# Sixteen chunks of score products split between TensorE and VectorE, and the softmax bias moved from GpSimd to ScalarE, in a two-layer decode kernel

## The chip, the cores and the metric

The kernel runs on one core of one Trainium2 chip. The metric is the device time of one execution in microseconds (us), smaller is better. Engines are named as in the profile: PE is TensorE, PEld its weight load, DVE is VectorE, ACT is ScalarE, POOL is GpSimd, SP is the engine that issues DMA transfers. L882 is line 882 of the kernel that the trace belongs to. All runs told of here gave correct results by the reference's tolerance and were in the fast state.

## The reference, cut to what matters

Two layers, each attention over a key/value cache followed by a small mixer MLP, for one new token of each of two sequences.

```python
B, Sq, D = 2, 1, 576;  H, Sk, Dh = 32, 16384, 128;  F = 4608      # all bf16
def A(x):                                    # attention
    q = (x @ wq).reshape(B, Sq, H, Dh).transpose(0, 2, 1, 3)
    scores = einsum("bhqd,bhkd->bhqk", q, k_cache) * Dh ** -0.5
    p = softmax(scores)
    return einsum("bhqk,bhkd->bhqd", p, v_cache)... @ wo
def B(x):                                    # MLP
    h  = gelu(layernorm(x) @ w1)
    hs = concatenate(shifted slices of h) @ w2     # every slice is shifted along S
    x1 = x + hs
    return x1 + gelu(layernorm(x1) @ w3) @ w4
for _ in range(2):
    x = x + A(layernorm(x));  x = x + B(layernorm(x))
```

With S = 1 every shift leaves zeros, so h is never used: the kernels compute it and multiply w2 by a zero tile. The weight of the problem is the cache: 64 pairs of batch and head, 4 MB of K and 4 MB of V each, read once per layer. I call one pair a unit; there are 128 units in a run.

## The kernel before: the parts that matter

A unit's 16,384 keys are 128 blocks of 128 keys, in 16 chunks of 8 blocks. K lies with the keys on the partitions, and the kernel's score matmul takes it with the head's 128 elements there, so each block is first transposed on TensorE into PSUM, copied to SBUF by VectorE or (every third chunk) ACT, and then used as the weights of a matmul with one column of q.

```python
def pe_transposes(pe, u, c):                 # chunk c of unit u
    ...
    for i in range(CH):                      # CH = 8
        ins = pe.transpose(self.tps[slot][:, i*128:(i+1)*128], self.kbuf[kslot][:, jj, :], self.ident)   # L808
def copy_chunk(eng, g, is_act):              # is_act for every third chunk
    ...
    if is_act: ins = eng.activation(out=self.ktsb[:, ks], in_=src, func=ACT.Copy)      # L863
    else:      ins = eng.tensor_copy(out=self.ktsb[:, ks], in_=src)                    # L866
def pe_scores(pe, g):
    ...
    for i in range(CH):
        ins = pe.matmul(self.sps[sb][:, j:j+1], lhsT=self.ktsb[:, ks, i], rhs=self.qt_sb[:, gu:gu+1], ...)  # L831
```

When a unit's scores are there, the softmax follows across four engines, and the product with V last:

```python
def dve_rowmax(dv, ul): ...                  # max along the free axis -> m_sb                       L873
def pool_allreduce(g_, ul):
    self.wt(g_, "sem_rmax", gu + 1)
    g_.partition_all_reduce(self.mall_sb[:, gu:gu+1], self.m_sb[:, gu:gu+1], channels=128, reduce_op=ROP.max) # L879
    self.wt(g_, "sem_pool", gu + 1)
    g_.tensor_scalar(out=self.bias_sb[:, gu:gu+1], in0=self.mall_sb[:, gu:gu+1], scalar1=-scale, ...)         # L882
def act_exp(act, ul):
    self.wt(act, "sem_bias", gu + 1)
    ...
    act.activation(out=self.p_sb[pb], in_=self.sps[sb][:, 0:NB], func=ACT.Exp,
                   bias=self.bias_sb[:, gu:gu+1], scale=scale, accum_out=self.l_sb[:, gu:gu+1])               # L892
def pe_pv(pe, ul): ...                       # 128 matmuls of V blocks with columns of p             L847
```

K and V come in halves of 2048 KB, two of each per unit, into four K slots and five V slots; each is asked for when its slot comes free.

## Time and profile before

| | before |
|---|---|
| median of the first 6 runs | 3765.46 us (3756.93 to 3771.26) |
| span of the traced run | 3765.6 us |
| busy: PE, DVE, ACT, POOL | 62%, 26%, 20%, 2% |
| DMA, mean over the span | 298 GB/s |
| one unit | 28.2 us |

The prediction below shows the busy shares, the chain and the three idle times that carry the argument. Three more lines complete them. From the page of the kernel before, the queue that carries K and V (packets, MB, share of the time of 16 DMA engines) and the largest group of instructions (busy us, mean ns | idle before):

```profile
q1 hardware_dynamic: 96520, 1116.54, 74.6%
...
L808 PE MATMUL tps<-ident,kbuf 128*128 128x128 bf16 x16384 | 1698.9, 267 | 22.7 <-issue 19.0
```

A quarter of the DMA's time is unused, and the transposes are by far the costliest work. A reader who stops here will want to take transposes off TensorE. The view of the one source line of the bias says otherwise (duration min/median/max, first and last start):

```profile
L882 POOLq MODIFY_POOL_CONFIG  x256: 82/83/85, 40.9 to 3699.9; - x128
L882 POOL TENSOR_SCALAR bias_sb<-mall_sb x128: 260/260/262, 48.6 to 3707.1; 128x1 f32<-128x1 f32 x128
```

The bias is 128 instructions of 0.26 us; in front of each stand two changes of the GpSimd's configuration of 0.08 us. The changes themselves look free. The first one starts at 40.9 us and the bias it belongs to at 48.6: what costs is the time after them, which no instruction shows. The gap is 11.0 us on average and lies between 7.06 and 14.02. The prediction and the expectations call such a change, with the gap behind it, a code change. That is my name for it: what GpSimd does in the gap no trace shows.

For the sums of the prediction the trace gives three times on VectorE: a reduce of 360 inputs takes 532 ns (L682), one of 320 takes 492 ns (L641), so 1 ns per input and some 170 ns fixed, and a copy of 1024 elements out of PSUM takes 692 ns (L866). It holds no multiply of the size that the change brings, so the prediction's times for that are my estimate; the measured ones stand with the result.

### The profile page before, as it was taken

Reading aid. Unit: us, or ns where it says so; the run is one execution under the profiler, and the core shown is the slowest. Engines: PE = TensorE matmul, PEld = TensorE weight load, DVE = VectorE, ACT = ScalarE, POOL = GpSimd, SP = SyncE. Lnnn points to the kernel's source line nnn. Section 1 sums busy time; section 2 is a strip of 40 time slices with the busy share of each in tenths; the row PEclk is TensorE's granted clock in tenths of the full one; section 3 lists DMA queues with packets and bytes.
Section 4 is the critical chain, followed back from the end, with each engine's and each line's share of the span. In section 5 each row is a group of like instructions: output and inputs, shape, how many; then the busy total and the mean of one; then the engine's idle time right before and its main releaser. Section 6 shows DMA issues by size and latency. Waiting matters only on the chain.

```text
span 3765.6 us, 107964 instructions
## 1 busy us (share of the span) xinstructions
PE 2324.8 (62%) x50634; PEld 2280.1 (61%) x50634; DVE 988.3 (26%) x1646; ACT 762.0 (20%) x962; POOL 88.1 (2%) x279
## 2 busy tenths in 40 slices
PE   5556666656656656656665665566566656566566
PEld 5556666656656656656555655566566656566565
DVE  2222222222222222222232222222222222222222
ACT  2112112212122112112121211221122122121121
POOL 0000000000000000000000000000000000000000
PEclk8666666666766666666566666666666666666675
DMA  9777776877777777777497877678777777777774
GB/s 399 314 291 290 303 316 273 319 317 304 312 294 294 305 298 291 297 308 292 167 414 293 318 297 304 272 294 318 297 295 301 291 297 313 308 289 306 302 292 151
DMA packets 96965, 1123.44 MB, mean 298 GB/s; under 512 B 8964, under 2 KB 28680, under 8 KB 28680
## 3 DMA queue, kind: packets, MB, share of 16 engines
q1 hardware_dynamic: 96520, 1116.54, 74.6%
q8 instruction: 397, 6.50, 0.7%
q14 instruction: 48, 0.39, 0.0%
HBM read 1116.51 MB, written 0.00 MB: 297 GB/s over the span
## 4 chain that ended last, share of the span: by engine, by line
PE 48%; issue 42%; ACT 4%; POOL 2%; DVE 2%; DMA 1%; POOLq 0%; ACTq 0%; SPq 0%
PE tps L808 27%; PE ops L847 11%; PE sps L831 8%; ACT ktsb L863 3%; POOL mall_sb L879 1%; DVE m_sb L873 1%; POOL bias_sb L882 1%; ACT p_sb L892 1%; DMA wring<-in_B_w_dram 1%; PE tps L506 1%; DVE ktsb L866 0%; DMA kbuf<-in_A_k_cache_dram 0%; PE mps L506 0%; PE sps L666 0%; POOLq L882 0%
## 5 line engine op out<-in xcount | busy, mean ns | idle before, releaser
L808 PE MATMUL tps<-ident,kbuf 128*128 128x128 bf16 x16384 | 1698.9, 267 | 22.7 <-issue 19.0
L866 DVE COPY ktsb<-tps 128x1024 bf16<-128x1024 bf16 x1366 | 931.7, 692 | 2594.1 <-PE tps L808 2591.8
L831 PE MATMUL sps<-qt_sb,ktsb 128*128 128x1 bf16 x16384 | 763.1, 167 | 1288.1 <-ACT ktsb L863 1264.2
L831 PEld LDWEIGHTS sps<-qt_sb,ktsb 128*128 128x128 bf16 x16384 | 730.4, 106 | 1315.5 <-ACT ktsb L863 1289.9
L808 PEld LDWEIGHTS tps<-ident,kbuf 128*128 128x128 bf16 x16384 | 1288.1, 120 | 28.3 <-issue 23.1
L863 ACT ACTIVATE ktsb<-tps 128x1024 bf16<-128x1024 bf16 x682 | 697.2, 1022 | 1107.9 <-PE tps L808 1107.9
L847 PE MATMUL ops<-p_sb,vbuf 128*128 128x1 bf16 x16384 | 443.1, 163 | 60.8 <-issue 42.9
L847 PEld LDWEIGHTS ops<-p_sb,vbuf 128*128 128x128 bf16 x16384 | 429.9, 97 | 65.5 <-issue 47.5
L892 ACT ACTIVATE p_sb<-sps,bias_sb 128x128 bf16<-128x128 f32 x128 | 47.0, 368 | 1776.0 <-POOL bias_sb L882 1776.0
L879 POOL PARTITION_ALL_REDUCE mall_sb<-m_sb x128 | 48.8, 382 | 2136.7 <-DVE m_sb L873 2136.7
L882 POOL TENSOR_SCALAR bias_sb<-mall_sb 128x1 f32<-128x1 f32 x128 | 33.3, 260 | 1411.7 <-issue 1411.7
L873 DVE TENSOR_REDUCE m_sb<-sps 128x1 f32<-128x128 f32 x128 | 36.4, 284 | 39.8 <-PE sps L831 39.7
L892 ACT ACTIVATION_READ_ACCUMULATOR p_sb<-sps,bias_sb 128x1 f32 x128 | 24.7, 193 | 0.0
L506 PE MATMUL tps<-gT_bf,wring 128*128 128x2 bf16 x288 | 19.2, 171 | 5.3 <-DVE gT_bf L395 3.7
L506 PE MATMUL tps<-otn_sb,wring 128*128 128x2 bf16 x256 | 17.1, 171 | 7.1 <-DVE otn_sb L727 7.1
L624 PE MATMUL sps<-xn,wring 128*128 128x2 bf16 (+1 forms) x320 | 9.3, 165 | 18.4 <-DVE xn L361 13.0
L624 PEld LDWEIGHTS sps<-xn,wring 128*128 128x128 bf16 (+1 forms) x320 | 8.9, 104 | 18.8 <-DVE xn L361 13.2
L337 ACT ACTIVATE rstd<-var,epsb 128x2 f32<-128x2 f32 x8 | 2.4, 296 | 83.3 <-DVE var L330 83.3
L506 PEld LDWEIGHTS tps<-gT_bf,wring 128*128 128x128 bf16 x288 | 13.3, 108 | 7.2 <-DVE gT_bf L395 3.9
L506 PEld LDWEIGHTS tps<-otn_sb,wring 128*128 128x128 bf16 x256 | 11.9, 108 | 8.2 <-DVE otn_sb L727 7.3
L506 PE MATMUL mps<-gT_bf,wring 128*64 128x2 bf16 x72 | 15.1, 210 | 0.0
L666 PE MATMUL sps<-xn,wring 128*128 128x2 bf16 (+1 forms) x360 | 10.1, 165 | 7.4 <-DVE xn L361 7.4
(80 smaller groups left out, 110.7 us busy)
## 6 DMA issues: line engine op xcount, KB each, us to landing
kbuf<-in_A_k_cache_dram SPq DMA_DIRECT2D x256, 2048.0 KB, 8.4
vbuf<-in_A_v_cache_dram SPq DMA_DIRECT2D x256, 2048.0 KB, 15.9
wring<-in_B_w_dram SPq DMA_DIRECT2D x12, 864.0 KB, 8.9
wring<-in_A_wo_dram SPq DMA_DIRECT2D x8, 1152.0 KB, 19.3
wring<-in_B_w_dram SPq DMA_DIRECT2D x8, 1152.0 KB, 5.4
wring<-in_A_wq_dram SPq DMA_DIRECT2D x8, 1024.0 KB, 9.7
wring<-in_B_w_dram SPq DMA_DIRECT2D x6, 576.0 KB, 5.5
wring<-in_A_wq_dram SPq DMA_DIRECT2D x2, 512.0 KB, 14.3
```

Of the source, the lines that this page charges most:

```text
L506: ins = pe.matmul(self.out_bank(t), lhsT=wap[0:kk, t * 128:t * 128 + kl], rhs=rhs_fn(k), start=(k == 0), stop=(k == nk - 1))
L624: ins = pe.matmul(parts[:, k * U + h * B:k * U + (h + 1) * B], lhsT=wap[0:kk, h * 128:(h + 1) * 128], rhs=self.xn[0:kk, k, :], start=True, ...
L666: ins = pe.matmul(parts[:, k * MB + m * B:k * MB + (m + 1) * B], lhsT=wap[0:kk, m * 128:(m + 1) * 128], rhs=self.xn[0:kk, k, :], start=Tru ...
L808: ins = pe.transpose(self.tps[slot][:, i * 128:(i + 1) * 128], self.kbuf[kslot][:, jj, :], self.ident[:, :])
L831: ins = pe.matmul(self.sps[sb][:, j:j + 1], lhsT=self.ktsb[:, ks, i, :], rhs=self.qt_sb[:, gu:gu + 1], start=True, stop=True)
L847: ins = pe.matmul(self.ops_[:, gu:gu + 1], lhsT=self.vbuf[vslot][:, jj, :], rhs=self.p_sb[pb][:, j:j + 1], start=(j == 0), stop=(j == NB - 1))
L863: ins = eng.activation(out=self.ktsb[:, ks, :, :], in_=src, func=ACT.Copy)
L866: ins = eng.tensor_copy(out=self.ktsb[:, ks, :, :], in_=src)
L873: dv.tensor_reduce(out=self.m_sb[:, gu:gu + 1], in_=self.sps[sb][:, 0:NB], axis=AX.X, op=ALU.max).then_inc(self.sems["sem_rmax"], 1)
L879: g_.partition_all_reduce(self.mall_sb[:, gu:gu + 1], self.m_sb[:, gu:gu + 1], channels=128, reduce_op=ROP.max).then_inc(self.sems["sem_po ...
L882: g_.tensor_scalar(out=self.bias_sb[:, gu:gu + 1], in0=self.mall_sb[:, gu:gu + 1], scalar1=-scale, scalar2=None, op0=ALU.mult).then_inc(se ...
L892: act.activation(out=self.p_sb[pb][:, :], in_=self.sps[sb][:, 0:NB], func=ACT.Exp, bias=self.bias_sb[:, gu:gu + 1], scale=scale, accum_out ...
```

## The change

Its intent is to take most of the transposes, copies and score matmuls off TensorE. Chunks 0 to 5 of each unit stay there. The other ten (80 blocks) are computed by VectorE: K, keys on partitions, times q in every partition, summed along the free axis. On the way the bias goes to ACT, exp splits in two (scores in PSUM, scores in SBUF), the two denominators are added once per layer on GpSimd, and the unused h branch moves to the layer's end. The core of the diff, cuts marked:

```diff
 def pool_allreduce(g_, ul):
     g_.partition_all_reduce(self.mall_sb[...], self.m_sb[...], channels=128, reduce_op=ROP.max)
-    self.wt(g_, "sem_pool", gu + 1)
-    g_.tensor_scalar(out=self.bias_sb[...], in0=self.mall_sb[...], scalar1=-scale, ...)
 def act_exp(act, ul):
+    self.wt(act, "sem_pool", gu + 1)
+    act.activation(out=self.bias_sb[...], in_=self.mall_sb[...], func=ACT.Copy, scale=-scale)
     self.wt(act, "sem_bias", gu + 1)
-    act.activation(out=self.p_sb[pb][:, :], in_=self.sps[sb][:, 0:NB], func=ACT.Exp, ..., accum_out=self.l_sb[...])
+    act.activation(out=self.p_sb[pb][:, 0:NBP],  in_=self.sps[sb][:, 0:NBP],   func=ACT.Exp, ..., accum_out=self.l_sb[...])
+    act.activation(out=self.p_sb[pb][:, NBP:NB], in_=self.s_dve[sb][:, 0:NBD], func=ACT.Exp, ..., accum_out=self.l2_sb[...])
+def dve_diag(dv, ul): ...      # ident * q  -> diag_sb
+def pe_qb(pe, ul): ...         # ones^T @ diag: q in every partition, PSUM
+def dve_qb_copy(dv, ul): ...   # -> qb_sb
+def dve_dots(dv, ul, h):       # the blocks of K half h that are VectorE's
+    kap = self.kbuf[kslot][:, jj0:jj0 + nblk, :]
+    qb_bc = bass.AP(..., ap=[partition, [0, nblk], row of 128])
+    dv.tensor_tensor(out=kap, in0=kap, in1=qb_bc, op=ALU.mult)
+    dv.tensor_reduce(out=self.s_dve[ss][:, ...], in_=kap, axis=AX.X, op=ALU.add)
+    dv.tensor_copy(out=self.junk1[...], in_=self.ident[:, 0:1])        # then frees the K half
 ... (row maximum of both parts; the K slot is free when both engines are done with it)
 def attn_normalize(self, l):
+    g.tensor_tensor(out=self.l_sb[...], in0=self.l_sb[...], in1=self.l2_sb[...], op=ALU.add)   # GpSimd, once per layer
     g.partition_all_reduce(self.den_sb[...], self.l_sb[...], channels=128, reduce_op=ROP.add)
 ... (w1, its layer norm and gelu: moved behind the end of the layer)
-KB(..., NKB=4, NVB=5, NW=5)
+KB(..., NKB=4, NVB=5, NW=5, NKT=4, NCP=6, ACT_COPY_EVERY=1)           # NCP: chunks left on TensorE
```

> **What bounds the kernel now.** I read the page's busy shares first, then the groups with their idle times, then the chain of waits over one unit, then the DMA rate by window. A unit is one batch and head: 128 of them, 64 in each of two layers. No engine is full:
>
> ```profile
> PE 2324.8 (62%) x50634; PEld 2280.1 (61%) x50634; DVE 988.3 (26%) x1646; ACT 762.0 (20%) x962; POOL 88.1 (2%) x279
> ...
> PE 48%; issue 42%; ACT 4%; POOL 2%; DVE 2%; DMA 1%; POOLq 0%; ACTq 0%; SPq 0%
> ...
> L831 PE MATMUL sps<-qt_sb,ktsb 128*128 128x1 bf16 x16384 | 763.1, 167 | 1288.1 <-ACT ktsb L863 1264.2
> ...
> L892 ACT ACTIVATE p_sb<-sps,bias_sb 128x128 bf16<-128x128 f32 x128 | 47.0, 368 | 1776.0 <-POOL bias_sb L882 1776.0
> ...
> L882 POOL TENSOR_SCALAR bias_sb<-mall_sb 128x1 f32<-128x1 f32 x128 | 33.3, 260 | 1411.7 <-issue 1411.7
> ```
>
> The reader is to see a chain of three idle times with the same count of about 128. TensorE waits 1264 us for an ACT copy; ACT stands 1776 us behind an exp that waits for the bias; the bias, a 0.26 us GpSimd multiply, starts after 1411.7 us of "issue", 11.0 us each time (1411.7 / 128). The chain of waits over one unit shows it in order:
>
> ```profile
> 1003.14 0.38 POOL mall_sb L879
> 1003.52 0.07 POOLq L882 x2
> 1003.59 11.35 issue
> 1014.94 0.27 POOL bias_sb L882
> ...
> 1015.70 0.92 ACT ktsb L863
> 1016.62 0.05 issue
> 1016.66 0.38 PE sps L831 x8
> ```
>
> The two queue entries in front of the gap are, in the view of that source line, MODIFY_POOL_CONFIG, 256 of them in the run[...]. Behind the late bias ACT, in order, holds up one copy out of PSUM, TensorE's score matmuls wait for that copy, and all stops for 11 to 12 us per unit.
>
> The first attention stretch runs from 26.8 us to the end of its last PV at 1833.2 us, the second from 1900.8 to 3711.5 us: 28.2 us per unit. TensorE is busy in only 16.5 us of such a unit, and so is the DMA for three quarters of it:
>
> ```profile
> 1000.00:1028.10 28.10, 16.54 (x391) 16.37 (x389) 6.98 (x11) 6.49 (x8) 0.64 (x2) 0.74 0.76 304
> ```
>
> ```profile
> 22.00:32.00 10.00, 9.78 (x243) 9.74 (x244) 3.51 (x8) 1.12 (x2) 0.00 (x0) 1.00 0.99 421
> 32.00:42.00 10.00, 9.63 (x232) 9.33 (x229) 6.98 (x11) 5.98 (x6) 0.38 (x1) 1.00 1.01 426
> ```
>
> The last two columns are DMA share and GB/s. With its queue full the DMA moves 421 to 426 GB/s, so 304 is no limit yet. It will be the next one.
>
> [...]
>
> **The change, part by part.** It keeps the first 6 of a unit's 16 chunks of keys on TensorE (transpose, copy, score matmul), all 6 copies now on ACT, and gives the other 10 chunks (80 blocks of 128 keys) to VectorE: multiply K in place by a broadcast q, then reduce. It moves the bias from GpSimd to ACT, splits exp in two, adds a diagonal and one matmul to broadcast q, and puts the unused h branch at the layer's end. The order of instructions shows that the GpSimd queue in a layer's loop is now 64 all-reduces and nothing else.
>
> GpSimd: 128 code changes of 11.0 us leave the loop. All of it was on the path. One pair remains per layer (a tensor_tensor on the denominators between two all-reduces), which costs what the last unit's pair costs now: 14.6 us from the all-reduce at 3699.5 to the reciprocal at 3714.1.
>
> TensorE per unit: 48 transposes and 48 score matmuls in place of 128 and 128. A chunk of both takes 0.65 us at the high clock and 1.06 us at the low one (successive transposes in the timeline), so 6 take 3.9 to 6.4 us; PV stays at 3.3 us; q's matmul 0.3 us. Sum 7.5 to 10 us.
>
> ACT per unit: 6 copies of 1.02 us, bias 0.25, two exps of about 0.3 with 0.19 for each accumulator: 7.4 us.
>
> VectorE per unit[...]: multiply of 2048 and 8192 elements[...] 1.22 and 4.42 us; reduces 2.28 and 8.68; two markers of one element 0.30; three small ops of row maximum 0.59; diagonal 0.19; copy of q from PSUM 0.28. Sum 17.96 us. Eleven gaps of 0.04 us between dependent ops (seen in the layer norm) and the trip to TensorE and back, 0.45 us, make 18.9 us. This is a serial loop: row maximum of one unit, q of the next, its dots.
>
> DMA per unit: four transfers of 2048 KB, 8.39 MB; at 424 GB/s 19.8 us.
>
> So the DMA, at 19.8, lies just above VectorE at 18.9, and TensorE and ACT are far below. Can the DMA be kept busy? The second K half is asked for when the dots of two units earlier end, and two V halves follow it at once: three transfers, 14.8 us. The first K half follows when its own dots and the sixth transpose are done, by my reckoning about 8 us later, well before those have drained. So yes.
>
> The sum. K/V of a layer: 64 x 19.8 = 1267 us, and 4.7 MB of wo in the same queue 11 us: 1278. Layer 1: K starts at 12 us, after wq; slower start (312 GB/s in 12 to 22 us) 3 us; last softmax 2 us: all-reduce at 1295; denominators to 1310. From there to the first K of layer 2, now 1835.9 to 1883.7: 48 us, so 1358. Layer 2: 1278 + 3 + 2 + 15 gives 2656. From there to the end, now 3714.1 to 3765.6: 52 us. **2708, say 2710 us.** The h branch leaves the middle of the layer but stays in order on the same engines ahead of the next norm and of the final cast, so I give it nothing.
>
> **Rivals.** (a) VectorE sets the pace: [...] Then 5.3 us more per unit, 24.2, and about 3270 us. [...] (b) VectorE's loop with its waits is nearer to 21 us, because the all-reduce, exp and q's trip add up more than I counted: about 2850. [...] (c) The gain is all from the code change that left GpSimd, and the offload to VectorE is hidden: TensorE's 16.5 us plus some 3 us of softmax wait would already sit near the DMA's 19.8. I believe this largely: it makes the same time, but says that the bias alone would bring nearly all of the gain. (d) The author's likely reason, that TensorE's transposes are the bound, gives 28.2 down to about 18.9; it makes no other time, since DMA then binds, but would leave the bias alone with little. The 11.35 us of issue speak against it.
>
> **Range and chances.** At 437 GB/s, the best rate in short slices of the trace, 1239 us per layer give about 2630. A loop of 21 us gives 2850. I take 2630 to 2850. Faster by over 2% is near certain (0.98): even (a) is faster by 13%. What is left is an unseen stall, 0.01 each.
>
> **What would show it.** In the new profile: no MODIFY_POOL_CONFIG in the loops and no 11 us issue gap before a bias; DMA share 0.95 or more at 415 to 430 GB/s through attention; multiplies of 8192 elements at 4.4 us and reduces at 8.7 us; VectorE busy about 18 us of 20 per unit, waiting for K where it waits; TensorE under half busy. A multiply of 8.7 us would be (a); DMA below 90% with VectorE never waiting for K would be (b); a code change still in the loop would break all of it.

## The result, and the profile after

The changed kernel takes 2724.86 us, the median of 8 runs (2723.14 to 2726.36), against 3761.82 us, the median of 16 runs of the kernel before. The ratio is 0.7243 (95% interval 0.7232 to 0.7255). Here and below a ratio is the mean time of one kernel's fast runs over that of the other's fast runs in the same rounds, so it is not quite the ratio of the medians quoted.

The page of the changed kernel, parts 1, 3, 4 and 5:

```profile
PE 1403.1 (52%) x30282; PEld 1358.1 (50%) x30282; DVE 2324.9 (85%) x1554; ACT 913.2 (34%) x1432; POOL 51.7 (2%) x155
...
q1 hardware_dynamic: 96520, 1116.54, 97.7%
...
DMA 66%; DVE 22%; PE 7%; issue 4%; SPq 0%; POOL 0%; ACT 0%; DVEq 0%; POOLq 0%
...
L924 PE MATMUL tps<-ident,kbuf 128*128 128x128 bf16 x6144 | 772.1, 305 | 407.7 <-DMA kbuf<-in_A_k_cache_dram 406.1
...
L978 PE MATMUL ops<-p_sb,vbuf 128*128 128x1 bf16 x16384 | 471.2, 165 | 629.5 <-DMA vbuf<-in_A_v_cache_dram 615.7
```

The bytes are the same as before; the share of DMA time that carries them rose from 74.6% to 97.7%. In the chain the 42% of issue have become 4%, and DMA, 1% before, is 66%. TensorE now waits for K and for V, not for a copy. One unit in the timeline (start us, duration us, engine, instruction, [idle before <- releaser]):

```profile
1004.55 0.35 POOL L1072 PARTITION_ALL_REDUCE mall_sb<-m_sb  x1 [19.22 <-DVE m_sb L1063]
...
1004.93 0.20 ACT L1080 ACTIVATE bias_sb<-mall_sb 128x1 f32<-128x1 f32 x1 [0.32 <-POOL mall_sb L1072]
1005.00 0.29 DVE L1015 CAST qb_sb<-mps 128x128 bf16<-128x128 f32 x1 [0.38 <-PE mps L962]
...
1005.38 1.23 DVE L1036 TENSOR_TENSOR kbuf<-kbuf,qb_sb 128x2048 bf16<-128x2048 bf16 x1
...
1006.65 2.29 DVE L1039 TENSOR_REDUCE s_dve<-kbuf 128x16 f32<-128x2048 bf16 x1
...
1009.17 4.42 DVE L1036 TENSOR_TENSOR kbuf<-kbuf,qb_sb 128x8192 bf16<-128x8192 bf16 x1
1013.63 8.69 DVE L1039 TENSOR_REDUCE s_dve<-kbuf 128x64 f32<-128x8192 bf16 x1
...
1021.03 1.03 PE L924 MATMUL tps<-ident,kbuf 128*128 128x128 bf16 x8 [3.04 <-DMA kbuf<-in_A_k_cache_dram]
...
1023.36 0.24 DVE L1052 TENSOR_REDUCE m_sb<-s_dve 128x1 f32<-128x80 f32 x1 [0.79 <-PE sps L949]
...
1024.13 0.35 POOL L1072 PARTITION_ALL_REDUCE mall_sb<-m_sb  x1 [19.23 <-DVE m_sb L1063]
```

From one all-reduce to the next are 19.58 us, against 28.2 before. This is a common unit and not the mean: after the first eight of a layer, every fourth or fifth one takes about 21 us or more, for a reason that was not looked into, and the mean of the first layer is 19.91 us ((1301.83 - 47.71) / 63, from its first and its last all-reduce). The bias starts 0.03 us after its all-reduce ends (1004.55 + 0.35 to 1004.93). VectorE is a serial loop that almost fills the unit; its longest wait here, 0.79 us, is for TensorE's scores, and TensorE had waited 3.04 us for a K half. So the DMA seems to set the pace, with VectorE right behind it; an experiment below tests that. Three of these units in the view by window (length, busy us of PE, PEld, DVE, ACT, POOL with instructions, granted clock, DMA share, GB/s):

```profile
1000.00:1060.00 60.00, 31.38 (x675) 30.47 (x675) 53.70 (x34) 21.06 (x33) 1.05 (x3) 0.56 1.01 426
```

One thing in the new trace the kernel before doesn't have. At the end of each layer's stream the DMA doesn't stop sharply. The DMA view of 1250 to 1330 us in 40 slices of 2 us:

```profile
DMA  9999999999999999999975445543000000059999
GB/s 442 434 426 418 442 426 410 385 410 434 418 434 426 434 410 434 434 426 422 387 303 221 205 205 221 205 187 129 31 0 0 0 0 0 0 115 438 406 414 419
```

All remaining V transfers had been asked for by 1272.5 us, yet the eight slices from 1290 to 1306 us have a mean of 210 GB/s, at about half of the DMA share. The packed trace says why. It keeps the times of the 16 landing signals of every transfer (no view lists them; there are 16 DMA engines). At 210 us the 16 signals of a V half come within 5 us of each other. (In the kernel before, with its DMA not full, those of the first layer's last V half come within 2 us.) For the last V half of the layer, eight come at 1289.2 to 1291.6 us and the other eight at 1303.6 to 1305.9. So half of the signals run ahead by 14 us at the end, and the tail is the other half finishing alone. That each eight belongs to eight engines is inferred; it fits the half share.

### The profile page after: what moved, and what is told of

It reads as the page before. It is cut to its first block, busy times and chain, and to the rows that moved or that the text cites. A ratio compares the mean times of both kernels' runs of the same rounds, so it can differ in the third digit from the quotient of the medians.

```text
span 2723.7 us, 66636 instructions
## 1 busy us (share of the span) xinstructions
PE 1403.1 (52%) x30282; PEld 1358.1 (50%) x30282; DVE 2324.9 (85%) x1554; ACT 913.2 (34%) x1432; POOL 51.7 (2%) x155
## 3 DMA queue, kind: packets, MB, share of 16 engines
q1 hardware_dynamic: 96520, 1116.54, 97.7%
## 4 chain that ended last, share of the span: by engine, by line
DMA 66%; DVE 22%; PE 7%; issue 4%; SPq 0%; POOL 0%; ACT 0%; DVEq 0%; POOLq 0%
DMA kbuf<-in_A_k_cache_dram 62%; DVE s_dve L1039 12%; DVE kbuf L1036 6%; DMA vbuf<-in_A_v_cache_dram 4%; PE tps L924 4%; PE sps L949 1%; DVE qb_sb L1015 1%; PE mps L962 1%; DVE diag_sb L1006 1%; DVE m_sb L1052 1%; PE tps L537 1%; DVE m_sb L1057 1%; DVE junk L1044 0%; PE mps L537 0%; DMA wring<-in_B_w_dram 0%
## 5 line engine op out<-in xcount | busy, mean ns | idle before, releaser
L1039 DVE TENSOR_REDUCE s_dve<-kbuf 128x16 f32<-128x2048 bf16 (+1 forms) x256 | 1404.4, 5486 | 8.8
L994 ACT ACTIVATE ktsb<-tps 128x1024 bf16<-128x1024 bf16 x768 | 780.6, 1024 | 1519.3 <-PE tps L924 1499.9
L924 PE MATMUL tps<-ident,kbuf 128*128 128x128 bf16 x6144 | 772.1, 305 | 407.7 <-DMA kbuf<-in_A_k_cache_dram 406.1
L924 PEld LDWEIGHTS tps<-ident,kbuf 128*128 128x128 bf16 x6144 | 593.6, 139 | 418.1 <-DMA kbuf<-in_A_k_cache_dram 416.1
L1036 DVE TENSOR_TENSOR kbuf<-kbuf,qb_sb 128x2048 bf16<-128x2048 bf16 (+1 forms) x256 | 723.3, 2825 | 12.9 <-issue 1.3
L949 PEld LDWEIGHTS sps<-qt_sb,ktsb 128*128 128x128 bf16 x6144 | 313.8, 114 | 1.5 <-ACT ktsb L994 1.4
L949 PE MATMUL sps<-qt_sb,ktsb 128*128 128x1 bf16 x6144 | 302.4, 170 | 0.6 <-ACT ktsb L994 0.5
L1052 DVE TENSOR_REDUCE m_sb<-s_dve 128x1 f32<-128x80 f32 x128 | 30.2, 236 | 145.1 <-PE sps L949 144.7
L1044 DVE CAST junk<-ident 128x1 f32<-128x1 bf16 x256 | 39.4, 154 | 27.2 <-DVE s_dve L1039 0.9
L1090 ACT ACTIVATE p_sb<-s_dve,bias_sb 128x80 bf16<-128x80 f32 x128 | 44.8, 350 | 0.0
L1086 ACT ACTIVATE p_sb<-sps,bias_sb 128x48 bf16<-128x48 f32 x128 | 38.6, 301 | 4.3
L537 PE MATMUL tps<-otn_sb,wring 128*128 128x2 bf16 x256 | 17.1, 171 | 19.9 <-DVE otn_sb L818 19.9
```

The source lines that it names most:

```text
L924: ins = pe.transpose(self.tps[slot][:, i * 128:(i + 1) * 128], self.kbuf[kslot][:, jj, :], self.ident[:, :])
L949: ins = pe.matmul(self.sps[sb][:, j:j + 1], lhsT=self.ktsb[:, ks, i, :], rhs=self.qt_sb[:, gu:gu + 1], start=True, stop=True)
L994: ins = eng.activation(out=self.ktsb[:, ks, :, :], in_=src, func=ACT.Copy)
L1036: dv.tensor_tensor(out=kap, in0=kap, in1=qb_bc, op=ALU.mult).then_inc(self.sems["sem_dotm"], 1)
L1039: dv.tensor_reduce(out=self.s_dve[ss][:, j0 - NBP:j1 - NBP], in_=kap, axis=AX.X, op=ALU.add).then_inc(self.sems["sem_dot"], 1)
L1052: i1 = dv.tensor_reduce(out=self.m2_sb[:, gu:gu + 1], in_=self.s_dve[sb][:, 0:NBD], axis=AX.X, op=ALU.max)
```

## The experiments

Each run is listed with the ratio to the kernel before of its own rounds.

| run | median us | ratio (95%) |
|---|---|---|
| the change, again, beside the next three | 2724.72 | 0.7254 (0.7237 to 0.7271) |
| before + bias on ACT | 2736.82 | 0.7287 (0.7267 to 0.7308) |
| the change without the offload | 2736.13 | 0.7284 (0.7267 to 0.7301) |
| the change with the bias on GpSimd | 2947.89 | 0.7842 (0.7817 to 0.7867) |
| the change, V transfers halved (wrong on purpose) | 2574.68 | 0.6845 (0.6823 to 0.6867) |
| before + bias on ACT, V transfers halved (wrong on purpose) | 2429.31 | 0.6458 (0.6437 to 0.6479) |
| the change, denominators added on VectorE | 2705.70 | 0.7193 (0.7175 to 0.7211) |
| the same, next layer's first K and V prefetched | 2716.15 | 0.7221 (0.7206 to 0.7236) |
| denominators on VectorE, 10 chunks on TensorE | 2717.49 | 0.7230 (0.7209 to 0.7252) |
| denominators on VectorE, 4 chunks on TensorE | 2965.15 | 0.7888 (0.7858 to 0.7918) |

The theory is rival (c) of the prediction: the gain comes from the configuration changes that left GpSimd, after which the DMA binds. Against it stands rival (d): the transposes were the bound, and the offload brings the gain. The first four runs, on one chip, are the two parts alone and together, and a control.

**The bias alone.** The kernel before, with nothing but the bias moved:

```diff
 # pool_allreduce
-    self.wt(g_, "sem_pool", gu + 1)
-    g_.tensor_scalar(out=self.bias_sb[...], in0=self.mall_sb[...], scalar1=-scale, ...)
 # act_exp
-    self.wt(act, "sem_bias", gu + 1)
+    self.wt(act, "sem_pool", gu + 1)
+    act.activation(out=self.bias_sb[...], in_=self.mall_sb[...], func=ACT.Copy, scale=-scale)
+    self.wt(act, "sem_bias", gu + 1)
```

> The kernel before with one edit: the bias is made on ACT (a Copy activation with scale) and no longer on GpSimd. Theory A (the code change on GpSimd is what the time went to, DMA is next): the 11 us issue gap goes, a unit takes the DMA's 19.6 us as it does in the changed kernel (TensorE needs 16.5 us plus about 1.5 us of softmax), DMA share near 1.0, and the layer's end saves its last code change too: 2680 to 2740 us. Theory B (TensorE's transposes are the bound, so the offload to VectorE is what pays): little changes, 3600 us or more. In between, TensorE in its serial order with the softmax wait takes more than the DMA, say 21 us a unit: 2880 us, and then the offload has a share.

Measured: 2736.82 us (2736.29 to 2737.77). Of the 1028.8 us that the whole change saves in these rounds (3753.54 - 2724.72), this one line saves 1016.7, which is 99%. From its timeline, and its view by window:

```profile
1034.90 0.35 POOL L879 PARTITION_ALL_REDUCE mall_sb<-m_sb  x1 [20.19 <-DVE m_sb L873]
1035.29 0.20 ACT L887 ACTIVATE bias_sb<-mall_sb 128x1 f32<-128x1 f32 x1 [1.41 <-POOL mall_sb L879]
```

```profile
1000.00:1060.00 60.00, 47.13 (x1139) 45.91 (x1136) 22.06 (x35) 17.59 (x25) 1.06 (x3) 0.77 1.00 424
```

The 11 us in front of the bias are gone, 0.04 us are left, and with all 256 transposes and score matmuls still on TensorE the DMA is full at 424 GB/s. TensorE, busy 47.13 of 60 us, has room. Rival (d) falls.

What fills the gap is not shown. The runs show that the gap comes and goes with the change between an all-reduce and a plain operation: 11.0 us, 128 times, in the kernel before, and none in this one's loop. The two queues of kind "instruction" moved 397 and 48 packets in the kernel before, and 397 and 44 here, so the DMA views show no traffic that goes with the 128 gaps.

**Everything but the offload.** The changed kernel with all 16 chunks on TensorE and the copies shared as before:

```diff
-KB(..., NKT=4, NCP=6,  ACT_COPY_EVERY=1)
+KB(..., NKT=4, NCP=16, ACT_COPY_EVERY=3)
```

> The changed kernel with all 16 chunks on TensorE and one copy in three on ACT, as before: everything of the change but the offload. Theory A: as the bias alone, 2680 to 2740 us, within 1% of that run; the moved h branch is worth nothing. Theory B: 3600 us or more. If the moved h branch had a price or a gain, it is the difference between this run and the bias alone.

Measured: 2736.13 us (2734.49 to 2736.94), within 0.7 us of the bias alone, with overlapping ranges. So the moved h branch, which is in this kernel and not in the other, is worth nothing that shows. (The two differ also in the buffers of transposed K, NKT=4 here and 5 there.)

**The offload without the bias.** The changed kernel with the bias back on GpSimd:

```diff
 # pool_allreduce
+    self.wt(g_, "sem_pool", gu + 1)
+    g_.tensor_scalar(out=self.bias_sb[...], in0=self.mall_sb[...], scalar1=-scale, ...)
 # act_exp
-    self.wt(act, "sem_pool", gu + 1)
-    act.activation(out=self.bias_sb[...], in_=self.mall_sb[...], func=ACT.Copy, scale=-scale)
```

> The changed kernel with the bias put back on GpSimd. Theory A: the code change is back, 11 to 14 us between all-reduce and bias; ACT's copies of chunks 2 to 5 wait behind it, TensorE's last scores come about 22 us after the row maximum before, so a unit takes 22 to 25 us: 3000 to 3400 us, and VectorE waits for TensorE's scores at the row maximum. Theory B: VectorE's dots hide it, 2725 us as the changed kernel.

Measured: 2947.89 us (2935.14 to 2950.86), below the range that was expected. Its timeline over one unit:

```profile
1008.99 0.38 POOL L1072 PARTITION_ALL_REDUCE mall_sb<-m_sb  x1 [9.57 <-DVE m_sb L1063]
1021.41 0.26 POOL L1075 TENSOR_SCALAR bias_sb<-mall_sb 128x1 f32<-128x1 f32 x1 [12.04 <-issue]
...
1031.24 0.38 POOL L1072 PARTITION_ALL_REDUCE mall_sb<-m_sb  x1 [9.57 <-DVE m_sb L1063]
```

and from its page the chain by engine and the group of the bias:

```profile
issue 53%; PE 31%; ACT 6%; DVE 6%; POOL 3%; DMA 1%; POOLq 0%; ACTq 0%; SPq 0%; DVEq 0%
...
L1075 POOL TENSOR_SCALAR bias_sb<-mall_sb 128x1 f32<-128x1 f32 x128 | 34.6, 270 | 1448.3 <-issue 1448.3
```

The gap is back, 1448.3 / 128 = 11.3 us each, and binds again: issue is 53% of the chain. (At this kernel's layer ends a plain operation, the sum of the denominators, follows a plain one, the bias, on GpSimd. It had no such gap: 1.8 us of waiting for ACT over both layers, and no issue.) The unit of 22.25 us (mean of the first layer 21.71) is the gap and the work that follows it in line. What the gap leaves out of the unit is smaller than before because TensorE has less to do: 30.79 us of 60 in this window, where the kernel before had 16.54 of 28.1. So with the gap in place the offload is worth 806 us (3753.54 to 2947.89), and with the gap away about 12 us (2736.82 to 2724.72). The gains of the two parts alone, 806 and 1017 us, don't add up to the 1029 of both, because each shortens the same line until the DMA stops it.

**The control.** The unedited change beside these three:

> The changed kernel unedited, on the same chip as the three others, so that they can be compared with it: 2725 us, ratio 0.724.

It ran at 2724.72 us (2724.46 to 2725.22), so the 12 us by which it beats the bias alone are real: the ranges don't touch.

**Is the DMA the bound?** V transfers after the first five are cut to half their size, in the changed kernel and in the one with only the bias moved. The second half of each V slot then holds old data, so both are wrong on purpose; they pass the tolerance all the same.

```diff
-    sp.dma_start(self.vbuf[slot][:, :, :], v_src(u, h))
+    nb = BP if kp < NVB else BP // 2
+    sp.dma_start(self.vbuf[slot][:, 0:nb, :], v_src(u, h)[:, 0:nb, :])
```

> The changed kernel with every V transfer after the first five cut to half its bytes (wrong results on purpose): 6.3 MB a unit in place of 8.4, so the DMA would need 14.8 us. If the DMA sets the pace of the changed kernel, VectorE's loop takes over at about 18.8 us a unit (19.57 less the 0.8 us in which it waits for scores behind a late K): about 2630 us, DMA near 335 GB/s. If VectorE sets the pace already, nothing moves: 2725 us.

> The kernel before with the bias on ACT and the same cut of V (wrong results on purpose). With the DMA's limit lifted to 14.8 us, TensorE sets the pace: 17 to 18 us a unit, 2420 to 2540 us. That would be below the changed kernel with the same cut, so the offload would be a longer path than the one it replaces. If TensorE's order with the softmax takes more than VectorE's 18.8 us, it comes out above 2630 us.

Measured: 2574.68 us for the change, 2429.31 us for the bias alone. Their views by window, the change first:

```profile
1000.00:1060.00 60.00, 29.66 (x677) 29.02 (x678) 57.19 (x39) 20.88 (x33) 1.31 (x4) 0.56 0.79 319
```

```profile
1000.00:1060.00 60.00, 54.73 (x1378) 54.29 (x1376) 26.68 (x42) 21.28 (x29) 1.05 (x3) 0.82 0.93 366
```

With a quarter of the bytes gone both kernels get faster, so the DMA did bind both. In the changed kernel VectorE takes over, busy 57.19 of 60 us, at 18.73 us from one all-reduce to the next (1003.54, 1022.28, 1041.01). In the other TensorE takes over, busy 54.73 of 60 us; its units vary (1012.48, 1030.42, 1047.41), with a mean of 17.81 us over the first layer. The kernel that leaves all scores on TensorE is now the faster by 145 us. So the offload replaced a TensorE loop of 17.8 us per unit by a VectorE loop of 18.7; both hide under the DMA's 19.9.

My 2630 us for the first of them was too high, because I had taken the one unit of 19.57 us for the mean. The first layer's last all-reduce came at 1228.34 us instead of 1301.83, 73.5 us earlier. The mean unit fell from 19.91 to 18.75 us, and 63 times 1.16 us is 73. For 128 units that makes 148 us, so an estimate of 2576 us where 2574.68 was measured.

**The configuration changes that are left.** The denominators are added on GpSimd between two all-reduces, once per layer. The layer's end in the changed kernel:

```profile
1301.83 0.35 POOL L1072 PARTITION_ALL_REDUCE mall_sb<-m_sb  x1 [18.38 <-DVE m_sb L1063]
...
1309.15 0.31 POOL L804 TENSOR_TENSOR l_sb<-l_sb 128x64 f32<-128x64 f32 x1 [6.98 <-issue]
1315.46 0.73 POOL L807 PARTITION_ALL_REDUCE den_sb<-l_sb  x1 [6.00 <-issue]
```

The edit adds them on VectorE:

```diff
-    self.inc(g.tensor_tensor(out=self.l_sb[...], in0=self.l_sb[...], in1=self.l2_sb[...], op=ALU.add), "pool_chain")
+    self.inc(dv.tensor_tensor(out=self.l_sb[...], in0=self.l_sb[...], in1=self.l2_sb[...], op=ALU.add), "dve_g")
```

> The changed kernel with the sum of the two denominator parts (once per layer) on VectorE and not on GpSimd, so that no code change is left at a layer's end: about 13 us saved twice, 2700 us, if the chain there sets the end; nothing if the MLP's weight transfers set it.

Measured: 2705.70 us (2705.16 to 2705.94), the fastest of all complete kernels here, 0.7% below the change (interval 0.7175 to 0.7211 against 0.7232 to 0.7255). The same stretch:

```profile
1302.06 0.35 POOL L1072 PARTITION_ALL_REDUCE mall_sb<-m_sb  x1 [18.38 <-DVE m_sb L1063]
...
1303.52 0.23 DVE L801 TENSOR_TENSOR l_sb<-l_sb 128x64 f32<-128x64 f32 x1 [1.55 <-ACT p_sb L1090]
1303.83 0.74 POOL L807 PARTITION_ALL_REDUCE den_sb<-l_sb  x1 [1.42 <-DVE l_sb L801]
```

Both gaps are gone and the denominators come 11.6 us earlier, but the time fell by 19 us and not by the 26 expected. The first K of layer 2 was asked for 9 us earlier (1354.89 instead of 1363.82): the last V half had not landed until 1305.7 us, and 10.70 us of the chain behind it are MLP weights. Part of what the gap cost was hidden under the tail of the stream.

**Filling the DMA in the MLP.** Between the layers the K/V queue stands. This kernel asks for the next layer's first unit of K and V and second unit of K before w3:

```diff
-    self.issue_loads([t["w2"]] + t["w3"] + ...)
+    self.issue_loads([t["w2"]])
+    K half 0, V half 0, K half 1, V half 1 of unit 0, both K halves of unit 1, of layer l + 1
+    self.issue_loads(t["w3"] + ...)
```

> The run before plus K of the next layer's units 0 and 1 and V of unit 0 (and V of 1 after wq) asked for before the MLP's weights, where the DMA now stands idle between the layers: a further 10 to 25 us less, 2675 to 2690 us. If the weights that now queue behind those loads are needed at once, the gain is given back: 2700 us.

Measured: 2716.15 us, 10 us slower than without, a miss. From the chain of waits in order of time:

```profile
1322.56 32.32 DMA wring<-in_B_w_dram
```

The MLP weights after w2 stood in the same queue behind 12.6 MB of K and V, and the chain waits 32.32 us for them, where it waits 10.70 in the kernel without the prefetch. Layer 2's first all-reduce came at 1406.34 us, 18 us later than without the prefetch (1388.32), and its last one still 10 us later (2658.06 and 2647.71). So the early K and V won back about 8 of the 18 us that the late weights cost.

**How many chunks on TensorE?** With the denominators on VectorE, 10 and 4 chunks in place of 6:

```diff
-KB(..., NKT=4, NCP=6,  ACT_COPY_EVERY=1)
+KB(..., NKT=4, NCP=10, ACT_COPY_EVERY=1)      # and NCP=4
```

> The changed kernel with the denominators' sum on VectorE and 10 of 16 chunks on TensorE (6 on VectorE): VectorE's loop falls to some 12.5 us a unit, TensorE's work rises to 13 us. If the DMA alone sets the pace, the time is that of 6 chunks with the same sum, 2706 us, within 0.5%; a faster end of each layer could save 3 us twice. If the closeness of VectorE's loop (18.7 us) to the DMA's 19.6 cost something, it is gone and the time falls by more than 1%, below 2680.

> The same with 4 chunks on TensorE and 12 on VectorE: 2048 elements more per unit cost VectorE 1.07 us of multiply and 2.13 of reduce, 21.9 us a unit, above the DMA: VectorE becomes the bound, 2705 + 128 x about 2 = 2960 us, DMA near 385 GB/s. If it stayed at 2705, VectorE's loop would not be where I place it.

Measured: 2717.49 us with 10 and 2965.15 us with 4. The view by window with 4 chunks:

```profile
1000.00:1060.00 60.00, 19.09 (x446) 18.52 (x443) 58.13 (x28) 12.02 (x20) 0.70 (x2) 1.00 0.94 390
```

VectorE binds, 58.13 of 60 us, at 21.94 us per unit. So 6 is the best of the four numbers that ran (4, 6, 10, 16): two fewer cost 260 us, four more 12. The 10-chunk run is within the 0.5% that the first theory allowed. The second, that VectorE's loop so close to the DMA's costs over 1%, falls.

**What stays open.** From 6 over 10 to 16 chunks on TensorE the time goes 2705.70, 2717.49, 2736.13 us, although the DMA is full in all three and no configuration change with its gap is left at the layers' ends. The whole 30 us lie in the K/V stream: in the kernel with 16 chunks the last V half of layer 1 landed at 1320.9 us, with 6 at 1305.7, and there are two layers. Two lines of the DMA view of 100 to 1200 us, with 6 chunks and with 16:

```profile
q1 hardware_dynamic: 35819, 465.68, 100.1%
q8 instruction: 98, 1.61, 0.6%
```

```profile
q1 hardware_dynamic: 35530, 461.57, 99.4%
q8 instruction: 163, 2.67, 1.0%
```

With 16 chunks the K/V queue moved 0.9% fewer bytes in the same time. On two streams of about 1280 us that is an estimated 23 of the 30 us. A part of it, an estimated 10 us (0.4% of the two streams), goes with the queue of kind "instruction": it takes 1.0% of the engines' time in place of 0.6%, in a kernel of 107,460 instructions in place of 66,628; with 10 chunks it is 0.8%, of 83,524. The two groups of landing signals also stand further apart at the end of layer 1: the first eight of the last V half are there by 1299.4 us and the last by 1320.9, where with 6 chunks it is 1293.0 and 1305.7. No run separated these parts or showed why the groups drift.

## Why the prediction was right, point by point

- **The bound.** The 11.0 us behind the configuration changes were it. Moving one line took 99% of the gain, and putting it back brought the gap back at 11.3 us. What sets the gap's length is not shown: the first one of each layer was 7.64 and 7.28 us while the DMA moved 416 and 424 GB/s, the one before the all-reduce of the denominators 6.06 and 6.02 us.
- **The next bound.** The DMA at 19.8 us per unit, at 424 GB/s; measured 19.91 on average, and 19.58 at 426 GB/s in the stretch shown. Its share of 0.95 or more was 0.977 over the whole run. The queue was kept full as reckoned.
- **VectorE.** A loop of 18.9 us; 18.73 when nothing else bound it. The multiplies of 2048 and 8192 elements, put at 1.22 and 4.42 us, took 1.23 and 4.42, the reduces 2.29 and 8.69 for 2.28 and 8.68. The multiply's predicted times had no trace behind them; measured, with K overwritten in place, they hold. The small parts: two markers 0.31 us (0.30), row maximum 0.60 (0.59), diagonal 0.25 (0.19), q's copy 0.29 (0.28), the trip to TensorE and back 0.38 (0.45). Rival (a), a multiply at half that rate, is refuted; so is (b), a loop near 21 us. Where VectorE waited, it was not for K itself but for TensorE's scores (144.7 us over the run, 110 times), which wait for K.
- **ACT.** 7.4 us per unit predicted, 7.1 measured (913.2 / 128, with the little that ACT does between the layers): copies of 1.02 us, the bias 0.20, the two exps 0.30 and 0.35, 0.19 for each accumulator.
- **Rival (c) and (d).** (c) said that the bias alone would do; it did. TensorE's 16.5 plus some 3 us came out at 17.8. (d) is refuted as the cause of this gain; the offload would have been worth 806 us only beside the gap.
- **The layer's end.** The remaining pair of configuration changes, 14.6 us to the reciprocal, was 14.4 (1301.83 to 1316.22). To the first K of layer 2: 48 us predicted, 47.6 measured. From the last denominators to the end: 52 and 51.6. The h branch: nothing, and nothing.
- **TensorE under half busy** just failed: 52%. The transposes' mean rose from 267 to 305 ns, at a granted clock of 0.546 over the run instead of 0.668, and I had allowed a low clock in the sum of 7.5 to 10 us (the kernel before took 1.06 us for a chunk at a granted clock of 0.50, 1000.00 to 1003.10 us, and 0.65 us at 1.00, 1020.85 to 1024.60 us); a unit holds 10.2 (31.38 / 60 of 19.58). The upper end of that sum is already half of 19.8, so the sign was set tighter than the sum.
- **The sum** was 15 us short: the last all-reduce of layer 1 was predicted at 1295 and came at 1301.8, 6.8 us late; in layer 2 the stretch from the first K request to the last all-reduce was predicted at 1283 us and took 1293.6 (1363.82 to 2657.39). The term that was mis-sized is "last softmax 2 us" behind a stream that ends at full rate. The stream ended at about 1306 us, not 1293, for the rate halves in its last 16 us (210 GB/s in place of 426 loses 8 us). And behind the last unit's first K half, landed at 1280 us, lies a whole VectorE unit, not 2 us. The two overlap, and the second sets the all-reduce. Eight signals of that K half came by 1265.9 us and the rest by 1279.9; had all come level, it would have been some 7 us earlier, an estimate that is as large as layer 1's shortfall. The 4 us more of layer 2 were not taken apart.

## What to carry to other kernels

An engine that is 2% busy can be the bound, as GpSimd was here with 1411.7 us of idle time in front of 128 instructions of 0.26 us: look for idle time whose releaser is "issue", at the same count as a loop's trips, before counting busy shares. When a large change brings a large gain, run its smallest part alone; here one moved instruction did 99% of it, and the rewrite around it, worth 806 us while that instruction was in the wrong place, was worth 12 us once it was not. And before shortening an engine's path ask which bound comes next: here it was the DMA, at 19.9 us per unit above both ways of computing the scores (17.8 and 18.7). And take a pace from the whole loop: one unit of 19.58 us stood here for a mean of 19.91, and a forecast built on it missed by 55 us.
